# An attention and two MoE layers on one core: two tokens of a head share a transpose and a score product, K and V lie in chunks of 120 and 108 rows

## The chip, the core and the metric

The kernel runs on one NeuronCore of a Trainium2 chip. Its engines are TensorE (PE; its weight loads are listed apart as PEld), VectorE (DVE), ScalarE (ACT), GpSimd (POOL) and SyncE (SP), which here only issues transfers; sixteen DMA engines move data between HBM and SBUF. The metric is device time in microseconds (us).

## The reference, cut to what matters

```python
def _attn_ref(q, k, v):                      # (8, 8, 576, 64): batch, head, token, D
    k_p = k.reshape(B, H, Sp, 8, D).mean(axis=3)     # 576 tokens pooled by 8: 72 rows
    v_p = v.reshape(B, H, Sp, 8, D).mean(axis=3)
    scores = scale * np.matmul(q, k_p.transpose(0, 1, 3, 2))
    attn = softmax(scores)
    return np.matmul(attn, v_p)
def reference(...):
    x = attn_out.transpose(0, 2, 1, 3).reshape(4608, 512)
    x = _moe_ref(x, ...)     # noisy top-2 gate of 8 experts, 512 -> 1024 -> 512, relu
    return _moe2_ref(x, ...) # h = x @ w_in; (h - tanh(h)) @ w_out, 512 -> 2048 -> 512
```

All arrays are float32. Every token's row passes through the two MoE layers by itself, so any order of the rows serves inside the kernel, as long as noise and output use the same one.

## The kernel before, in words

The program has three stages, one after another on TensorE: attention (`attention`, about the first 210 us of the span), the experts (`moe`) and the last layer (`Moe2`). The two MoE stages run in float16 pairs.

Attention is written out by hand, in one order for every engine (there is no scheduler). The 4608 tokens make 36 tiles of 128; a pair of batches is 9 tiles, and the fifth of them lies across both. A loop of steps runs over the tiles, and step t holds one stage of several tiles, in this order: `st_exps(t)` (ACT, one exponential for each head, L1370), `st_norm(t - 1)` (DVE), `st_g(t - 4)` (DVE: the output row `xr`, L1430, and the gate's logits `lg`, L1438, both out of the PSUM tile `px`), `st_attT(t - 2)` (PE transposes, L1395, and ACT copies, L1396), `st_q(t + 2)` (PE transposes, L1344, and an ACT copy, L1346), `st_scores(t + 1)` (PE, L1354, and the DVE maximum `mx`, L1357), the work that prepares a batch (below), and `st_av(t - 3)` (PE, L1413, into `px`). Between them `tick` puts in DVE work of the gate. An engine runs its instructions in the order in which they are written. An f32 product or transpose counts as two PE instructions in the trace.

**Scores.** `st_q` transposes a tile's q two heads at a time: 64 values of one head and 64 of the next make the 128 columns. The block `kb` of a batch holds the pooled K, with rows 0 to 63 filled for even heads and 64 to 127 for odd ones and zero elsewhere, so that one product of 144 columns gives the scores of both heads.

**Pooling.** The 576 rows of a batch (8 heads of 72) lie in five chunks of 128, 128, 128, 96 and 96 rows, each row with its 8 tokens side by side. Three additions halve them (L1171: 4, 2, 1 tokens), then `kbd` (L1331) multiplies each chunk by `parity`, an identity whose columns are zeroed by the head's parity, and one ACT copy brings the result to `kb` (L1334).

**Output.** `st_av` multiplies the transposed weights by `vb`, which holds for each chunk up to three heads of 64 + 16 columns (V and V times the gate's weights). A PSUM bank of `px` takes four heads, so chunk 2, which holds rows of heads 3, 4 and 5, is split into a product of one head (80 columns) and one of two:

```python
for g, parts in enumerate((((0, 0, 2), (1, 0, 3), (2, 0, 1)), ((2, 1, 2), (3, 0, 2), (4, 0, 2)))):
    for i, (c, j, w) in enumerate(parts):
```

`st_g` reads both banks with one instruction for `xr` and one for `lg`.

**Transfers.** `load_q` (L1187) brings a tile's q, 1024 runs of 256 bytes, four tiles ahead. K and V of batches 0 and 1 come whole (`load_kv`, L1153); later ones in halves, of which the second is added on arrival by POOL's queue (`load_half`, L1163 and L1165). At the start DVE builds `parity` (L1220 to L1225) and small constants, and `warm` lets PE multiply zeros (L1200) so that its clock is up.

Of the kernel before, what the change touches and what calls it, by code (L numbers as in the profile page):

```python
# [37 lines left out]
def kernel(ctx, tc, q, k, v, w_gate, w_noise, noise, w1, w2, w_in, w_out, out):  # L38
# [57 lines left out]
    z.run(ctx)  # L96

# [561 lines left out]
class Moe2:  # L659
# [165 lines left out]
    def main(self, near):  # L825
# [225 lines left out]
        def L2(j, f, blocks=range(4)):  # L1051
# [9 lines left out]
            if f == KF - 1:  # L1061
                for i in blocks:
# [6 lines left out]
                    r = 128 * (4 * j + i)  # L1069
                    nc.sync.dma_start(self.out[r:r + 128, :], o)  # L1070
# [57 lines left out]
def attention(nc, tc, st, V):  # L1128
# [13 lines left out]
    KV = {}  # L1142


    cuts = (0, 128, 256, 384, 480, 576)
# [23 lines left out]
    def add(e, b, nm, n, c=slice(0, 5)):  # L1169
        a = KV[b, nm]  # L1170
        e.tensor_add(a[:, c, 0:n], a[:, c, 0:n], a[:, c, n:2 * n])  # L1171

    QL = {}
# [37 lines left out]
    KB = [one.tile([128, 2 * HP * SP], F32, name=f"kb{i}") for i in range(2)]  # L1211
    VB = [one.tile([128, 5, 3, D + 2 * E], F32, name=f"vb{i}") for i in range(2)]

    of = one.tile([128, 5, 4], F32, name="of")
    odd = one.tile([128, 5, 2], F32, name="odd")
    lt = one.tile([128, 5, 4], F32, name="lt")
    for c0, c1, step, base in ((0, 3, 128 - 2 * SP, 2 * SP), (3, 5, 96 - 2 * SP, cuts[3] - 4 * SP)):
        nc.gpsimd.iota(of[:, c0:c1], pattern=[[step, c1 - c0], [-SP, 4]], base=base, channel_multiplier=1,
                       allow_small_or_imprecise_dtypes=True)
# [17 lines left out]
    load_q(2)  # L1237
    load_kv(1, "k")
    load_kv(0, "v", each)
    load_q(3)  # L1240
    for w, o in ((w_gate, 0), (w_noise, E)):
        nc.sync.dma_start(wg[:, 0:H, o:o + E], w.rearrange("(h p) e -> p h e", p=64))
    load_kv(1, "v")
    nz = ep.tile([128, NT, E], F32, name="nz")
    for c in each:
        add(nc.vector, 0, "k", 4, slice(*c))
# [3 lines left out]
    nc.vector.memset(zero8, 0.0)  # L1250
# [7 lines left out]
    for c0, c1, base, step in ((0, 1, 0, 0), (1, 4, 56, -16), (4, 5, 48, 0)):  # L1258
# [8 lines left out]
    def prep_jobs(b, first=False):  # L1267
# [94 lines left out]
    def st_exps(t):  # L1362
# [8 lines left out]
        if t % 4 == 3:  # L1371
            SM[1] = sm, t0
# [436 lines left out]
```

## Time and profile before

| | |
|---|---|
| three runs | 1750.15, 1753.28, 1758.94 us (median 1753.28) |
| the profiled execution | 1757.43 us, of which its span 1755.6 |
| PE, DVE, ACT, POOL busy | 98%, 72%, 53%, 16% of the span |
| PE busy in 0 to 15, 15 to 30, 75 to 150, 150 to 210 us | 11.16 of 15, 10.37 of 15, 71.69 of 75, 57.47 of 60 us |
| DMA share in 45 to 60, 75 to 150, 150 to 210 us | 1.18, 1.00, 0.48 |

A DMA share is the mean busy share of the sixteen engines, where packets that overlap on an engine count twice. PE's busy time counts the whole length of a product, and lengths overlap, so a PE that is busy may still be waiting a little.

### The profile page before, as it was taken

The numbers are of one execution on the slowest core, as the hardware profiler recorded it, in microseconds if no ns is written. First come the engines' busy times: TensorE is split into PE (matmuls) and PEld (weight loads), VectorE is DVE, ScalarE is ACT, GpSimd is POOL, SyncE is SP. The second block draws the span as 40 slices with busy tenths as digits, with TensorE's granted clock in tenths as the row PEclk, the third lists the DMA queues.
The fourth block names the chain that finished last, engine by engine and source line by source line (L and its number), as shares of the span: only waits on it lengthen the run. The fifth ranks groups of instructions, "written<-read, shape, count | busy, mean of one in ns | idle before, by whom it ended". The sixth has DMA issues, their size and how long they took to land.

```text
span 1755.6 us, 28446 instructions
## 1 busy us (share of the span) xinstructions
PE 1723.1 (98%) x10574; PEld 1040.4 (59%) x10576; DVE 1266.2 (72%) x2547; ACT 922.9 (53%) x2229; POOL 274.7 (16%) x267
## 2 busy tenths in 40 slices
PE   7999999999999999999999999999999999999997
PEld 5989855454454545445454544666666666666664
DVE  5789788766666676666564558688787978888775
ACT  5788634435243443434343446656575756657553
POOL 2443113131030301101010211102010101200000
PEclk9999999999999999999999999999999999999999
DMA  9998335645746464535643445223131304232100
GB/s 222 271 192 214 103 106 165 165 132 150 184 124 181 137 175 132 126 120 131 170 131 88 124 125 127 68 53 85 43 87 35 97 19 97 66 50 64 22 25 26
DMA packets 271413, 203.35 MB, mean 116 GB/s; under 512 B 188512, under 2 KB 222816, under 8 KB 271264
## 3 DMA queue, kind: packets, MB, share of 16 engines
q1 hardware_dynamic: 251808, 155.09, 33.9%
q0 software_dynamic: 19200, 45.89, 11.4%
q8 instruction: 85, 1.39, 0.3%
q14 instruction: 64, 0.52, 0.1%
q10 hardware_dynamic: 256, 0.46, 0.1%
HBM read 121.82 MB, written 45.74 MB: 95 GB/s over the span
## 4 chain that ended last, share of the span: by engine, by line
PE 91%; DMA 3%; DVE 3%; ACT 2%; SPq 1%; issue 1%; ACTq 0%; DVEq 0%
PE pt L917 10%; PE ph L356 7%; PE ph L917 7%; PE ph L358 7%; PE ph L357 7%; PE py L1058 7%; PE py L1059 7%; PE py L1060 7%; PE py L378 7%; PE py L379 7%; PE py L380 7%; PE px L1413 3%; PE py L385 1%; PE psc L1354 1%; DMA qt<-in_q 1%; DMA xTp<-xp 1%
## 5 line engine op out<-in xcount | busy, mean ns | idle before, releaser
L360 ACT ACTIVATE hT<-ph 128x512 f16<-128x512 f32 (+2 forms) x192 | 96.4, 504 | 400.3 <-PE ph L358 390.6
L356 PE MATMUL ph<-xTp,pair 128*128 128x384 f16 (+2 forms) x736 | 245.4, 333 | 2.9 <-DMA xTp<-xp 2.9
L357 PE MATMUL ph<-xTp,pair 128*128 128x384 f16 (+2 forms) x736 | 244.9, 333 | 0.0
L358 PE MATMUL ph<-xTp,pair 128*128 128x384 f16 (+2 forms) x736 | 244.9, 333 | 0.0
L361 DVE SCALAR_TENSOR_TENSOR hT<-ph,hT 128x512 f16<-128x512 f32 (+2 forms) x192 | 110.6, 576 | 182.8 <-ACT hT L360 181.1
L1060 PE MATMUL py<-wo,gT 128*128 128x512 f16 x576 | 218.3, 379 | 1.2 <-DVE gT L1007 1.2
L1058 PE MATMUL py<-wo,gT 128*128 128x512 f16 x576 | 218.3, 379 | 0.0
L378 PE MATMUL py<-pair,hT 128*128 128x512 f16 x576 | 218.3, 379 | 0.0
L380 PE MATMUL py<-pair,hT 128*128 128x512 f16 x576 | 218.3, 379 | 0.0
L379 PE MATMUL py<-pair,hT 128*128 128x512 f16 x576 | 218.3, 379 | 0.0
L1059 PE MATMUL py<-wo,gT 128*128 128x512 f16 x576 | 218.3, 379 | 0.0
L917 PEld LDWEIGHTS <-wi 128*128 128x128 f16 x1536 | 150.2, 98 | 58.5 <-DMA y<-yp 0.3
L315 POOL DMA_INDIRECT xg<-x_d,idx x75 | 79.1, 1055 | 653.1 <-DVE xp L342 480.8
L730 POOL DMA_INDIRECT y<-y_d,ridx x64 | 79.2, 1238 | 518.6 <-DVE y L741 278.2
L356 PEld LDWEIGHTS <-pair 128*128 128x128 f16 x768 | 75.0, 98 | 75.7 <-issue 12.9
L358 PEld LDWEIGHTS <-pair 128*128 128x128 f16 x768 | 75.1, 98 | 56.5
L357 PEld LDWEIGHTS <-pair 128*128 128x128 f16 x768 | 75.1, 98 | 56.0 <-issue 0.2
L1017 ACT ACTIVATE th<-th,bias 128x512 f32<-128x512 f32 x144 | 102.5, 712 | 3.4 <-DVE th L1015 3.2
L1018 DVE SCALAR_TENSOR_TENSOR th<-th,t 128x512 f32<-128x512 f32 x144 | 98.3, 683 | 1.4 <-ACT th L1017 1.4
L1014 DVE SCALAR_TENSOR_TENSOR t<-hb,cinf,hs 128x512 f32<-128x512 f32 x64 | 47.9, 749 | 71.0 <-ACT hs L1013 71.0
L1007 DVE TENSOR_TENSOR gT<-th,gT 128x512 f16<-128x512 f32 x144 | 98.4, 683 | 0.2 <-ACT gT L1006 0.2
L1060 PEld LDWEIGHTS <-gT 128*128 128x128 f16 x576 | 56.3, 98 | 69.5 <-DVE gT L1007 1.7
(319 smaller groups left out, 3415.6 us busy)
## 6 DMA issues: line engine op xcount, KB each, us to landing
stage<-in_moe_w SPq DMA_DIRECT2D x64, 512.0 KB
y_d<-ys SPq DMA_DIRECT2D x82, 256.0 KB
x_d<-xr SPq DMA_DIRECT2D x36, 256.0 KB
out<-o SPq DMA_DIRECT2D x36, 256.0 KB
qt<-in_q SPq DMA_DIRECT2D x32, 256.0 KB
raw<-in_moe_w_in SPq DMA_DIRECT2D x32, 256.0 KB
raw<-in_moe_w_out SPq DMA_DIRECT2D x32, 256.0 KB
ws_d<-ys SPq DMA_DIRECT2D x16, 256.0 KB
```

Source lines behind the costliest of these rows:

```text
L356: nc.tensor.matmul(p[:, :nt], w[:, 0, m, s], x[:, 0, m, :nt], start=(m == 0), stop=False)
L357: nc.tensor.matmul(p[:, :nt], w[:, 0, m, s], x[:, 1, m, :nt], start=False, stop=False)
L358: nc.tensor.matmul(p[:, :nt], w[:, 1, m, s], x[:, 0, m, :nt], start=False, stop=(m == KD - 1))
L361: stt(h[:, 1, :nt], p[:, :nt], 0.0, h[:, 0, :nt], op0=OP.max, op1=OP.subtract)
L378: nc.tensor.matmul(p, h[:, 0, s], w[:, 0, f], start=(f == 0), stop=False)
L379: nc.tensor.matmul(p, h[:, 0, s], w[:, 1, f], start=False, stop=False)
L380: nc.tensor.matmul(p, h[:, 1, s], w[:, 0, f], start=False, stop=(f == KF - 1))
L917: nc.tensor.matmul(p, w[:, a, m], y[:, c, b, m], start=(start and m + x == 0), stop=(m == 1 and x == 2), skip_group_check=True)
L1017: nc.scalar.activation(q, q, AF.Square, bias=bias[:, 2:3], scale=SP5)
L1058: nc.tensor.matmul(p, g[:, 0, s], wo[:, 0, f], start=(f == 0), stop=False)
L1059: nc.tensor.matmul(p, g[:, 0, s], wo[:, 1, f], start=False, stop=False)
L1060: nc.tensor.matmul(p, g[:, 1, s], wo[:, 0, f], start=False, stop=(f == KF - 1))
```

## The change

Four things are changed, all in attention, with what they bring along at the two ends (the order of the tokens).

- **Tokens.** Four neighbouring tokens of a head are read as one run of 1024 bytes: partition p of a group holds tokens 4p to 4p + 3. Tiles 0 to 3 and 5 to 8 of each nine are such groups; tile 4 is read as before. So the tokens of a tile are now every fourth one of 512, and output rows (`token_rows`) and noise follow.
- **Scores.** A transpose takes two neighbouring tokens of one head instead of two heads of one token, and the product gives the scores of both tokens by that head's K. The even tile of a pair does heads 0 to 3 for both tokens, the odd tile heads 4 to 7; the weights of both tiles are complete after the second. `kb` now holds all heads twice, once in rows 0 to 63 and once in rows 64 to 127, with zeros that POOL writes once; ACT copies one half and DVE the other. `parity` is gone.
- **Chunks.** They have 120, 120, 120, 108 and 108 rows: 360 rows are five heads, so chunks 0 to 2 fill one bank with heads 0 to 4 and chunks 3 and 4 the other with heads 5 to 7. The product of one head is gone; `st_g` takes two instructions for `xr` and two for `lg`. Three chunks of a load now have 120 rows and two have 108.
- **Start.** The first K additions stand ahead of DVE's constants; V of batch 0 is loaded ahead of K of batch 1; fewer products of zeros; the first additions of batch 1 come one step later.

```diff
+def token_rows(a, t):
+    g, u = divmod(t, 9)
+    r = 1152 * g + (512 if u == 4 else 640 * (u > 4))
+    if u == 4:
+        return a[r:r + 128, :]
+    return a[r:r + 512, :].rearrange("(p i) d -> p i d", i=4)[:, u % 5, :]
...
-    cuts = (0, 128, 256, 384, 480, 576)
+    cuts = (0, 120, 240, 360, 468, 576)
...
-    def load_q(t):
-        qt = ld.tile([128, H, D], F32, name="qt", bufs=4)
+    def load_q4(t, h=slice(0, H), i=slice(0, 4)):
+        b, s = divmod(t * 128, S)
+        if t not in QG:
+            QG[t] = ld.tile([128, H, 4, D], F32, name="qt4", bufs=2)
+            for j in range(4):
+                QL[t + j] = QG[t][:, :, j]
+        nc.sync.dma_start(QG[t][:, h, i], q[b, h, s:s + 512, :].rearrange("h (p i) d -> p h i d", i=4)[:, :, i])
...
-    warm(22)
-    for nm in "kv":
-        for i in range(2):
-            nc.gpsimd.memset(KVT[nm][i][96:128, 3:5], 0.0)
+    warm(18)
     load_kv(0, "k", each, (nc.sync, nc.scalar))
-    load_q(0)
-    load_q(1)
+    load_q4(0, i=slice(0, 2))
+    KB = [one.tile([128, 20 * SP], F32, name=f"kb{i}") for i in range(2)]
+    for t in KB2:
+        nc.gpsimd.memset(t[64:128, 0], 0.0)
+        nc.gpsimd.memset(t[0:64, 1], 0.0)
+    def pads(nm, i):
+        nc.gpsimd.memset(KVT[nm][i][96:128], 0.0)
+    for nm, i in (("v", 0), ("k", 1), ("v", 1)):
+        pads(nm, i)
...
-    parity = one.tile([128, 5, 2, 128], F32, name="parity")
-    tt(parity, identf[:, None, None, :].to_broadcast([128, 5, 2, 128]), odd[:, :, :, None].to_broadcast([128, 5, 2, 128]), op=OP.mult)
+    for c in each:
+        add(nc.vector, 0, "k", 4, slice(*c))
...
-                        nc.tensor.matmul(p[64 * i:64 * i + 64, c - c0], KV[b, "k"][:w, c, 0], parity[:w, c, i, 0:w],
+                        nc.tensor.matmul(p[64 * i:64 * i + 64, c - c0], KV[b, "k"][:w, c, 0], identf[:w, 0:w],
                                          start=True, stop=True, skip_group_check=True)
-                o = KB[b % 2][:, cuts[c0]:cuts[c1]].rearrange("p (c n) -> p c n", n=w)
-                nc.scalar.activation(o, p, AF.Copy, scale=1.0 / 512)
+                o = KB2[b % 2][:, :, cuts[c0]:cuts[c1]].rearrange("p i (c n) -> p i c n", n=w)
+                nc.scalar.activation(o[0:64, 0], p[0:64], AF.Copy, scale=1.0 / 64)
+                ts(o[64:128, 1], p[64:128], 1.0 / 64, None, op0=OP.mult)
...
-                    nc.tensor.matmul(p[o:o + n, 2 * m:2 * m + 2].rearrange("p h s -> p (h s)"),
-                                     QT[t][:, 2 * g + m, o:o + n], KB[b % 2][:, 2 * SP * (2 * g + m):2 * SP * (2 * g + m + 1)], start=True, stop=True)
+                        h = SP * (HP * (t - a) + 2 * g + m)
+                        kb = KB2[b % 2][:, :, h:h + SP]
+                    nc.tensor.matmul(x, QT[t][:, 2 * g + m, o:o + n], kb, start=True, stop=True)
...
-        if t % 4 == 0:
-            SM[0] = wk.tile([128, 4, 2, 4], F32, name="sm"), t
+        if t % 9 in (0, 4, 5):
+            SM[0] = wk.tile([128, 4, H], F32, name="sm"), t
...
-            for g, parts in enumerate((((0, 0, 2), (1, 0, 3), (2, 0, 1)), ((2, 1, 2), (3, 0, 2), (4, 0, 2)))):
+            for c in range(5):
+                r, h, w = cuts[c + 1] - cuts[c], hb[c] - 5 * (c > 2), 2 + (c == 1)
+                nc.tensor.matmul(p[c > 2][o:o + n, n1 * h:n1 * (h + w)], a[:r, c, o:o + n],
...
+        for h, x, r in gs:
+            tt(xr.rearrange("p (h n) -> p h n", n=D)[:, h], x[:, :, 0:D], r.to_broadcast([128, x.shape[1], D]), op=OP.mult)
...
+    def load_nz():
+        n, o = noise.rearrange("(g s) e -> s g e", s=2 * S), nz.rearrange("p (g t) e -> p g t e", t=9)
+        for t, s in ((0, 0), (5, S + 64)):
+            for g in range(B // 2):
+                nc.sync.dma_start(o[:, g, t:t + 4], n[s:s + 512, g].rearrange("(p i) e -> p i e", i=4))
+        nc.sync.dma_start(o[:, :, 4], n[512:640])
...
-            load_q(t + 4)
+        for u, h in ((t + 6, slice(0, 4)), (t + 5, slice(4, 8))):
+            if 5 < u < NT and u % 9 in (0, 5):
+                load_q4(u, h)
+        if 4 < t + 4 < NT and (t + 4) % 9 == 4:
+            load_q1(t + 4)
...
-            warm((4, 2, 6, 4)[t])
+            warm((3, 0, 2, 0)[t])
```

DVE at the start of the program, before, from its first instruction after two constants down to the last addition of batch 0's K (`kt`):

```order
L1220 TENSOR_SCALAR lt<-of 128x20
L1221 TENSOR_SCALAR of<-of 128x20
L1222 TENSOR_TENSOR of<-of,lt 128x20
L1225 TENSOR_TENSOR parity<-identf,odd 128x1280
L1227 TENSOR_SCALAR before<-rowi 128x128
L1232 MEMSET idx 128x288
L1171 TENSOR_TENSOR kt_109<-kt_109 128x256 x5
L1250 MEMSET zero_202 128x8
L1453 MEMSET mb_213 128x44
L1171 TENSOR_TENSOR kt_109<-kt_109 128x5x128
L1171 TENSOR_TENSOR kt_109<-kt_109 128x5x64
```

and after, down to the first maxima (`mx`), the additions of batch 0's V (`vt`) and the first constant:

```order
L1182 TENSOR_TENSOR kt_109<-kt_109 120x256 x3
L1182 TENSOR_TENSOR kt_109<-kt_109 108x256 x2
L1182 TENSOR_TENSOR kt_109<-kt_109 120x3x128
L1182 TENSOR_TENSOR kt_109<-kt_109 108x2x128
L1182 TENSOR_TENSOR kt_109<-kt_109 120x3x64
L1182 TENSOR_TENSOR kt_109<-kt_109 108x2x64
L1344 TENSOR_SCALAR kb_141<-pt 64x360
L1344 TENSOR_SCALAR kb_141<-pt 64x216
L1386 TENSOR_REDUCE mx<-psc 128x4 x4
L1182 TENSOR_TENSOR vt_111<-vt_111 128x256 x5
L1182 TENSOR_TENSOR vt_111<-vt_111 128x5x128
L1182 TENSOR_TENSOR vt_111<-vt_111 128x5x64
L1292 TENSOR_REDUCE vm<-vt_111 128x1
L1272 TENSOR_SCALAR lm<-hm 128x15
```

The additions of K moved ahead of every constant (the constants now stand behind V's additions), `parity` with its four small steps is gone, and two DVE copies to `kb` stand between the additions and the first maxima.

SP's queue at the start, before, from the first loads of q (`qt`) on:

```order
L1187 DMA qt<-in_q 128x8x64 x3
L1153 DMA kt_110<-in_k 128x3x512
L1153 DMA kt_110<-in_k 96x2x512
L1153 DMA vt_111<-in_v 128x512 x3
L1153 DMA vt_111<-in_v 96x512 x2
L1187 DMA qt<-in_q 128x8x64
L1242 DMA wg<-in_moe_w_gate 64x8x8
L1242 DMA wg<-in_moe_w_noise 64x8x8
L1153 DMA vt_112<-in_v 128x3x512
L1153 DMA vt_112<-in_v 96x2x512
L1187 DMA qt<-in_q 64x8x64 x2
L1187 DMA qt<-in_q 128x8x64
```

and after:

```order
L1201 DMA qt_139<-in_q 128x8x128 x2
L1161 DMA vt_111<-in_v 120x512 x3
L1161 DMA vt_111<-in_v 108x512 x2
L1161 DMA kt_110<-in_k 120x3x512
L1161 DMA kt_110<-in_k 108x2x512
L1252 DMA wg<-in_moe_w_gate 64x8x8
L1252 DMA wg<-in_moe_w_noise 64x8x8
L1206 DMA qt<-in_q 64x8x64 x2
L1201 DMA qt_179<-in_q 128x8x256
L1161 DMA vt_112<-in_v 120x3x512
L1161 DMA vt_112<-in_v 108x2x512
```

Tiles 0 to 3 of q now come with the first two loads and tiles 5 to 8 in one (L1201), both ahead of the last V; V of batch 0 stands ahead of K of batch 1.

DVE in the step of tile 7, where K of batch 2 is copied to `kb`, before:

```order
L1171 TENSOR_TENSOR kt_109<-kt_109 128x5x64
L1430 TENSOR_TENSOR xr<-px,rc 128x512
L1438 TENSOR_TENSOR lg<-px,rc 128x128
L1357 TENSOR_REDUCE mx<-psc 128x4 x2
L1171 TENSOR_TENSOR vt_111<-vt_111 128x5x64
L1283 TENSOR_REDUCE vm<-vt_111 128x1
```

and after:

```order
L1182 TENSOR_TENSOR kt_109<-kt_109 128x5x64
L1460 TENSOR_TENSOR xr<-px,rc 128x320
L1460 TENSOR_TENSOR xr<-px,rc 128x192
L1467 TENSOR_TENSOR lg<-px,rc 128x80
L1467 TENSOR_TENSOR lg<-px,rc 128x48
L1386 TENSOR_REDUCE mx<-psc 128x4 x2
L1344 TENSOR_SCALAR kb_141<-pt 64x360
L1344 TENSOR_SCALAR kb_141<-pt 64x216
L1182 TENSOR_TENSOR vt_111<-vt_111 128x5x64
L1292 TENSOR_REDUCE vm<-vt_111 128x1
```

A tile has two instructions more (`xr` and `lg` by bank), and in the step that builds `kb` two copies stand behind the maxima.

## Rows read from the trace of the kernel before

**Rows 1.** The page: span, and busy time of each engine.

```profile
span 1755.6 us, 28446 instructions
...
PE 1723.1 (98%) x10574; PEld 1040.4 (59%) x10576; DVE 1266.2 (72%) x2547; ACT 922.9 (53%) x2229; POOL 274.7 (16%) x267
```

**Rows 2.** Four stretches: length, busy PE, PEld, DVE, ACT, POOL, PE clock, DMA share, GB/s.

```profile
15.00:30.00 15.00, 10.37 (x62) 7.90 (x61) 9.13 (x19) 10.43 (x55) 0.00 (x0) 0.89 1.03 233
14.84:36.34 21.50, 16.71 (x126) 13.40 (x127) 14.34 (x32) 14.47 (x77) 4.26 (x4) 0.92 1.09 214
75.00:150.00 75.00, 71.69 (x614) 67.17 (x613) 62.32 (x172) 63.02 (x293) 34.71 (x37) 0.98 1.00 223
61.00:210.00 149.00, 142.92 (x1206) 134.39 (x1207) 123.11 (x345) 120.75 (x561) 51.56 (x59) 0.99 0.81 192
```

**Rows 3.** Chain of waits, 0 to 61 us: start, length, what.

```profile
20.49 7.75 DMA qt<-in_q
...
48.37 12.74 DMA qt<-in_q
```

**Rows 4.** Waits of PE, 12 to 61 us: total, times, longest.

```profile
PE pt L1344 <- DMA qt<-in_q: 4.6, 2, 2.4
```

**Rows 5.** The same, 61 to 210 us.

```profile
PE pt L1344 <- DMA qt<-in_q: 1.4, 1, 1.4
```

**Rows 6.** Timeline, 0 to 12 us: start, length, engine, line.

```profile
6.89 1.49 DVE L1225 TENSOR_TENSOR parity<-identf,odd 128x1280 f32<-128x1280 f32 x1
...
8.91 1.71 DVE L1171 TENSOR_TENSOR kt<-kt 128x256 f32<-128x256 f32 x5
```

**Rows 7.** Timeline, 12 to 36 us.

```profile
12.12 1.21 PE L1331 MATMUL pt<-parity,kt 128*64 128x128 f32 x20 [2.61 <-DVE kt L1171]
...
14.14 1.15 PE L1354 MATMUL psc<-kb,qT 128*128 128x144 f32 x8
...
28.38 0.63 PE L1344 MATMUL pt<-identf,qt 128*128 128x128 f32 x4 [2.41 <-DMA qt<-in_q]
...
33.10 1.48 DVE L1171 TENSOR_TENSOR vt<-vt 128x1280 f32<-128x1280 f32 x1
...
35.39 0.95 DVE L1357 TENSOR_REDUCE mx<-psc 128x4 f32<-128x288 f32 x2 [0.81 <-PE psc L1354]
```

**Rows 8.** Chain of waits, 61 to 206 us: share of each line.

```profile
by line: PE px L1413 30.8%; PE psc L1354 11.4%; DMA qt<-in_q 8.8%; PE pt L1395 8.5%; ACT at L1370 8.0%; PE pt L1344 5.0%; PE pt L1303 4.3%; PE pt L1331 3.2%; DVE xr L1430 2.5%; DVE mx L1357 1.9%; issue 1.8%; ACT aT L1396 1.8%; PE pt L1539 1
```

**Rows 9.** Chain of waits, 144 to 168 us.

```profile
150.06 2.77 PE px L1413 x24
...
154.94 1.72 PE px L1413 x12
...
157.21 0.44 PE pt L1344 x4
...
164.67 1.24 PE pt L1303 x10
```

**Rows 10.** Timeline of DVE, 204.9 to 207 us: a tile whose banks are read apart.

```profile
205.11 0.75 DVE L1430 TENSOR_TENSOR xr<-psc,rc 128x256 f32<-128x256 f32 x2
205.78 0.34 DVE L1438 TENSOR_TENSOR lg<-psc,rc 128x64 f32<-128x64 f32 x2
```

**Rows 11.** Timeline of DVE, 103.5 to 104.5 us: a tile before.

```profile
103.61 0.69 DVE L1430 TENSOR_TENSOR xr<-px,rc 128x512 f32<-128x512 f32 x1 [0.50 <-PE px L1413]
104.22 0.28 DVE L1438 TENSOR_TENSOR lg<-px,rc 128x128 f32<-128x128 f32 x1
```

**Rows 12.** Groups of DVE, 0 to 220 us: count, busy, mean ns, idle before.

```profile
L1430 DVE TENSOR_TENSOR xr<-px,rc 128x512 f32<-128x512 f32 x34 | 23.4, 688 | 13.4 <-PE px L1413 12.6
```

**Rows 13.** Copies of ACT to `kb`, 0 to 220 us.

```profile
L1334 ACT ACTIVATE kb<-pt 128x384 f32<-128x384 f32 x8 | 3.9, 491 | 9.0 <-PE pt L1331 9.0
```

**Rows 14.** DMA, 30 to 150 us: packets, and the queue of SP.

```profile
DMA packets 46214, 28.27 MB, mean 236 GB/s; under 512 B 29833, under 2 KB 42230, under 8 KB 46198
...
q1 hardware_dynamic: 39818, 21.88, 71.2%
```

More of the change, by code (lines that the diff above doesn't have):

```diff
@@ L1170, in add @@
         a = KV[b, nm]
-        e.tensor_add(a[:, c, 0:n], a[:, c, 0:n], a[:, c, n:2 * n])
-    QL = {}
+        whole = (b, nm) != (0, "k")
+        for c0, c1 in [(c.start, c.stop)] if whole else [s for s in ((c.start, min(c.stop, 3)), (max(c.start, 3), c.stop)) if s[0] < s[1]]:
+            w = 128 if whole else cuts[c1] - cuts[c1 - 1]
+            e.tensor_add(a[:w, c0:c1, 0:n], a[:w, c0:c1, 0:n], a[:w, c0:c1, n:2 * n])
+    QL, QG = {}, {}
     def runs(t):
@@ L1209, in attention @@
+    for t in KB2:
+        nc.gpsimd.memset(t[64:128, 0], 0.0)
+        nc.gpsimd.memset(t[0:64, 1], 0.0)
+    VB = [one.tile([128, 5, 3, D + 2 * E], F32, name=f"vb{i}") for i in range(2)]
+    def pads(nm, i):
+        nc.gpsimd.memset(KVT[nm][i][96:128], 0.0)
+    for nm, i in (("v", 0), ("k", 1), ("v", 1)):
+        pads(nm, i)
     rowi = one.tile([128, 128], F32, name="rowi")
     nc.gpsimd.iota(rowi, pattern=[[1, 128]], base=0, channel_multiplier=-1, allow_small_or_imprecise_dtypes=True)
-    KB = [one.tile([128, 2 * HP * SP], F32, name=f"kb{i}") for i in range(2)]
@@ L1212, in attention @@
[L1212 to L1219, printed above, removed]
@@ L1236, in attention @@
     nc.gpsimd.iota(lane, pattern=[[0, 1]], base=0, channel_multiplier=1, allow_small_or_imprecise_dtypes=True)
-    load_q(2)
+    load_q4(0, i=slice(2, 4))
+    load_kv(0, "v", each)
     load_kv(1, "k")
-    load_kv(0, "v", each)
-    load_q(3)
     for w, o in ((w_gate, 0), (w_noise, E)):
         nc.sync.dma_start(wg[:, 0:H, o:o + E], w.rearrange("(h p) e -> p h e", p=64))
+    load_q1(4)
+    load_q4(5)
     load_kv(1, "v")
     nz = ep.tile([128, NT, E], F32, name="nz")
-    for c in each:
-        add(nc.vector, 0, "k", 4, slice(*c))
     head = ep.tile([128, NT, 2, 2], F16, name="head")
@@ L1257, in attention @@
     lm = one.tile([128, 5, 3], F32, name="lm")
-    for c0, c1, base, step in ((0, 1, 0, 0), (1, 4, 56, -16), (4, 5, 48, 0)):
+    for c0, c1, base, step in ((0, 1, 0, 0), (1, 4, cuts[1] - SP, cuts[1] - 2 * SP), (4, 5, cuts[4] - 6 * SP, 0)):
         nc.gpsimd.iota(hm[:, c0:c1], pattern=[[step, c1 - c0], [-SP, 3]], base=base, channel_multiplier=1,
@@ L1362, in st_exps @@
     def st_exps(t):
-        at = wk.tile([128, 2, 4, SP], F32, name="at", bufs=3)
-        if t % 4 == 0:
-            SM[0] = wk.tile([128, 4, 2, 4], F32, name="sm"), t
+        a = both_of(t)
+        if t % 9 in (0, 4, 5):
+            SM[0] = wk.tile([128, 4, H], F32, name="sm"), t
         sm, t0 = SM[0]
-        AT[t] = at
+        if a != t - 1:
+            for u in (t,) if a is None else (t, t + 1):
+                AT[u] = wk.tile([128, H, SP], F32, name="at", bufs=4)
         for g, (p, mx) in enumerate(SC.pop(t)):
             for j in range(4):
-                nc.scalar.activation(at[:, g, j], p[:, j], AF.Exp, bias=mx[:, j:j + 1], accum_out=sm[:, t - t0, g, j:j + 1])
-        if t % 4 == 3:
-            SM[1] = sm, t0
+                u, h = (t, 4 * g + j) if a is None else (a + j % 2, HP * (t - a) + 2 * g + j // 2)
+                nc.scalar.activation(AT[u][:, h], p[:, j], AF.Exp, bias=mx[:, j:j + 1], accum_out=sm[:, u - t0, h:h + 1])
+        if t % 9 in (3, 4, 8):
+            SM[1 + t] = sm, t0
     def st_norm(t):
-        if t % 4 != 3:
+        if t % 9 not in (3, 4, 8):
             tick(2)
             return
-        sm, t0 = SM.pop(1)
+        sm, t0 = SM.pop(1 + t)
+        sm = sm[:, 0:t + 1 - t0]
         ts(sm, sm, 1e-9, None, op0=OP.add)
         tick()
-        rc = wk.tile([128, 4, H], F32, name="rc")
-        nc.vector.reciprocal(rc, sm.rearrange("p t a b -> p t (a b)"))
+        rc = wk.tile([128, 4, H], F32, name="rc", bufs=3)[:, 0:t + 1 - t0]
+        nc.vector.reciprocal(rc, sm)
         for u in range(t0, t + 1):
@@ L1616, in attention, with consts @@
         at(0, add, nc.vector, 0, "v", 4, slice(*c))
+    at(0, pads, "k", 0)
     at(0, P[0]["v2"])
     at(0, P[0]["v1"])
+    def consts():
+        head_mask()
+        nc.vector.memset(wg[:, H:], 0.0)
+        ts(before, rowi, 0.0, None, op0=OP.is_gt)
+        nc.vector.memset(ones, 1.0)
+        nc.vector.memset(idx, 0)
+        nc.vector.memset(zero8, 0.0)
+        for m in mb:
+            nc.vector.memset(m, 0.0)
+    at(0, consts)
     at_pe(1, P[0]["vt"])
```

87 lines of the change are left out of this document (43 added, 44 removed).

## The prediction

> **What bounds the kernel now.** I read the page first: PE is busy for 98% of a span of 1755.6 us [rows 1], so a change pays only where PE waits or where PE's own work shrinks. The change touches attention, the first 210 us, and leaves the 1545 us behind it as they are; those are PE's, so that what attention gains or loses arrives at the end one for one. The profiled execution took 1757.43 us, 1.8 outside its span. The sum is made against it; the median of the three runs is 4.15 us (0.24%) lower, and the forecast is moved down by that.
>
> Next the stretches [rows 2]. From 61 to 210 us PE is busy 142.92 of 149 us, DVE 123.11 and ACT 120.75: PE leads, two others are close behind. From 14.84 to 36.34 PE has 16.71 of 21.5, DVE 14.34, ACT 14.47: nobody is full, all wait. For whom is in the chain of the first 61 us: a q load from 20.49 on (7.75 us) and another from 48.37 (12.74 us) [rows 3]. PE stood 4.6 us in two waits for q there [rows 4] and 1.4 in a third just after [rows 5]. The DMA share is 1.03 to 1.09 in these stretches and 1.00 from 75 to 150 us, but 0.81 over 61 to 210 [rows 2]. So the start is set by transfers and by DVE's order, the rest mostly by PE: in the later chain the product with V holds 30.8%, five more PE lines 32%, all exponentials 8.0% [rows 8].
>
> **The change part by part.**
>
> *First scores.* DVE builds `parity` from 6.89 on and comes to K's additions only at 8.91, where it then waits for nothing [rows 6]; PE gets the pooled K at 12.12 and the first scores run at 14.14 [rows 7]. With the constants behind them the additions can begin when K lands. That is between no gain and some 3 us: 2.0 from 6.89 to 8.91, and the small steps ahead of `parity`. The two copies to `kb` now stand one behind the other (DVE's waits for ACT's), about 0.5 us more [rows 13], and the first q load has 512 instead of 256 KB, at 233 GB/s [rows 2] 1.1 us more. I take 1.5 us: first scores at about 12.6.
>
> *Steps 0 to 4.* Before, step 2 stood until tile 4's q was there: its transposes ran at 28.38 [rows 7]. Now tiles 0 to 3 come with the first loads and tile 4 needs no place behind K and V of batch 1 and a third tile. Once q no longer holds, the engines' work does: 14.34 us of DVE between the first maxima (14.84) and those of tile 4 (end 36.34), to which the moved constants (1.5 us) and the copies to `kb` (0.8) come, and from which V's first addition of batch 1 goes, 1.48 us [rows 7], since it now stands behind tile 4's maxima. That makes 15.2 us; with some 3 us for PE and ACT, which have 14 to 17 us of their own in turn, 18. From 13.3 on this ends at 31.3, 5 us ahead. The postponed addition is still to be done, and DVE has room for it after step 4, so I count a gain of **4.5 us** for both parts (from 2, if K's landing and PE's clock hold it, to 7.5). The granted clock is 0.89 from 15 to 30 us [rows 2], where PE waits most; fifteen products of zeros less are a risk there, fewer waits the opposite.
>
> *Third wait for q.* A tile's q is 1024 runs of 256 bytes; SP's queue took 71.2% of sixteen engines for 120 us with 39818 packets, 34 ns each [rows 14], so a tile costs at most 2.2 us of all engines. As 256 runs of 1 KB at the mean 236 GB/s it costs 1.1. With a group loaded five steps ahead the third wait goes: **1.4 us** (0 to 1.4). 32 tiles save some 1 us each of transfer, which is worth nothing by itself: nothing else in the chain after 61 us is a transfer.
>
> *Product with V.* The one-head product goes, two PE instructions of 80 columns. A tile's twelve take 1.72 us for 960 columns [rows 9]; by columns the two are 0.14, by number 0.29. Transposes of 128 columns take 0.11 each (four in 0.44) and products of 48 columns 0.124 (ten in 1.24), so that a narrower one is no cheaper: I take 0.22 a tile. Tiles across two batches have 24 shorter ones in 2.77, so their parts lose 0.18. All in all 32 x 0.22 + 8 x 0.18 = 8.4 us of PE. After 61 us 30.8% of 145 us = 44.7 us of this product are on the chain, 26 tiles' worth, so at most 5.7 us. DVE and ACT are 20 us behind over 149, unevenly: in steps where one of them leads, PE's saving becomes a wait. I take **4.5 us** (2 to 6.7).
>
> *Two more DVE instructions a tile.* Read apart, two banks took from 205.11 to 206.12 [rows 10]; read together, from 103.61 to 104.50 [rows 11]: 0.12 more, at most 0.34 if each added one costs half of the pair's 0.34. Over 34 tiles 4.1 us. The first of them still waits for all five products, as the order of the program has it, so nothing begins earlier. DVE idles before this instruction anyway, 12.6 us in 34 tiles for the product with V [rows 12], and that covers it where PE leads. `xr` is 2.5% of the later chain, 3.6 us, five tiles; with PE faster it will be there more often: **1 us** lost (0.6 to 4; without the cover up to 11.6).
>
> *`kb` by DVE.* Two copies for a batch, some 0.8 us by the 0.69 us that 512 elements out of PSUM take [rows 11]. They wait for PE's products and for ACT's copy before them: ACT's own wait there is 9.0 us in 8 batches [rows 13], with its 0.49 us copy about 1.6. Behind them on DVE stand V's last addition, the gate's steps and the next tile's `xr`, which waits for PE in most steps. For six batches 14 us at worst, nothing at best; I take the copies of two batches, **1.5 us**. ACT's part is as long as before (as many elements in a row).
>
> *The rest.* Three more sums and reciprocals a kernel (a new one after 4, 1 and 4 tiles), 0.3 us. The scores have as many columns as before, the transposes too; 36 output stores keep 2 KB rows; nine noise loads instead of one pass SP's queue ahead of the q group for tile 9, which is needed four steps later. POOL's longer zero fills stand ahead of V's and the second K's loads, and I take them to be over when SP comes there. All that I cost at nothing.
>
> Sum: -4.5 - 1.4 - 4.5 + 1.0 + 1.5 + 0.3 = **-7.6 us**, 1749.8 for the profiled execution and 1745.7 against the median, 0.43% less. I take 0.5%, about 9 us, for what a measurement here can tell from no change.
>
> **The rivals.**
>
> *DVE becomes the bound (slower).* From 61 to 210 us it has 123.11 us of work [rows 2]. The added work is 29 x 0.12 + 6 x 0.8 + 1 = 9.3 us, the waits of the copies 6 x 1.6 = 9.6: 142, against PE's 142.92 less 6.7. If the copies' waits are not hidden, DVE leads in most steps, the saving of PE is lost and 14 to 18 us come instead: with the start's 5.9 us gained, some +10 us, 1763. It decides from the point at which a step's DVE work, wait included, passes PE's, about 4.7 us a tile. For it: DVE is in order, and the copy waits for an engine that has a step's work ahead of it. Against it: DVE idles 12.6 us before `xr`, and only six steps have the copies.
>
> [...]
>
> *More than forecast.* If first scores come the full 3 us earlier and the steps take what DVE has to do, the start gives 8 to 9 us; if PE stays the leader in each step, the product gives 6.7 and the DVE terms fall to 1: -14 us, 1739. For it: both losses lie in idle time that the trace shows.
>
> **How the numbers follow.** The forecast (1741 to 1750) gets 0.50, a little less than half of it beyond 0.5%; more than forecast 0.22; transfers still set the start 0.15; DVE the bound 0.13. So faster 0.45, same 0.42, slower 0.13. The range reaches from the best case with every term at its end (-15 us, and 2 us for the median of a few runs: 1736) to the second rival and some of the way to the first, 1757; what is left out is the first rival's end and a little below.
>
> **What would show it.** First scores near 12.6 us; no PE wait for q in the first 61 us; tile 4's maxima near 31 us; ten PE instructions for the product with V in about 1.5 us where PE leads; `kb` copies on DVE with a wait of 1 to 2 us for ACT; attention's last `xr` about 7 us earlier, and the rest as long as before. Wrong it would be by a granted clock below 0.9 in the start, by K and V landing later, or by DVE idle moving from `xr` into `kb`.

## The result, and the profile after

The changed kernel took 1765.83 us (median of 6 runs, 1761.05 to 1769.22) beside 1754.02 for the kernel before on the same chip: ratio 1.0070, 95% interval 1.0052 to 1.0089. It is slower by 0.7%, by the ratio 12.3 us (9.1 to 15.6), where 0.43% faster was forecast. The profiled execution took 1766.92 us, 1.8 outside its span.

The page of the changed kernel, span and busy time of each engine (to be held against [rows 1]):

```profile
span 1765.1 us, 28281 instructions
...
PE 1723.4 (98%) x10481; PEld 1037.4 (59%) x10481; DVE 1274.9 (72%) x2634; ACT 922.7 (52%) x2229; POOL 286.0 (16%) x269
```

PE has 93 matmuls less and is busy as long as before. The work behind attention is as before; up to the last tile's transposed weights in attention (`aT` of tile 35, at 221.73 us here and 206.01 before) PE is busy 189.15 us at a mean granted clock of 0.95, where it was 188.45 at 0.98: what was taken out came back as time in which the same work ran slower. Where, the stretches say (length, busy PE, PEld, DVE, ACT, POOL, PE clock, DMA share, GB/s; the second runs from the first maxima to those of tile 4):

```profile
15.00:30.00 15.00, 10.65 (x78) 8.43 (x77) 12.93 (x40) 10.34 (x55) 0.00 (x0) 0.89 0.95 223
13.12:32.59 19.47, 15.12 (x116) 12.03 (x115) 15.01 (x44) 14.32 (x76) 1.36 (x1) 0.91 0.96 225
45.00:60.00 15.00, 10.54 (x80) 8.87 (x79) 6.29 (x19) 8.21 (x42) 6.26 (x6) 0.90 1.11 289
75.00:150.00 75.00, 63.91 (x490) 58.37 (x490) 57.45 (x173) 53.00 (x242) 30.94 (x33) 0.91 0.90 195
61.00:210.00 149.00, 130.74 (x1022) 119.86 (x1022) 123.75 (x373) 111.30 (x527) 54.06 (x59) 0.94 0.78 184
```

The start came near the forecast: the stretch from the first maxima to tile 4's is 19.47 us long instead of 21.50; it begins 1.72 us sooner and ends 3.75 us sooner [rows 2], where 5 were forecast for its end. The loss lies behind it. From 75 to 150 us PE, DVE and ACT are all less busy than before, by 8, 5 and 10 us, and the PE clock is 0.91 instead of 0.98 [rows 2]. All three waiting more suggests that something outside them is late. The DMA share fell too, from 1.00 to 0.90, and the GB/s from 223 to 195, so that the transfers look less loaded than before. That is the row that misleads here, as the experiments show.

The chain of waits of the changed kernel, 0 to 61 us, and under it from 61 to 100 (start, length, what):

```profile
7.72 6.05 DMA vt<-in_v
...
22.98 11.37 DMA vt<-in_v
...
44.24 11.15 DMA x_d<-xr
```

```profile
67.25 3.27 SPq L1206
...
70.57 9.76 DMA qt<-in_q
```

Before, two loads of q stood in the first 61 us [rows 3]. Now it is V twice, then the store of tile 0's x, which took 11 us to land and which `xr` of tile 3 waits for (three buffers). Behind 61 us stands the load of q for tile 13, the tile without a neighbour (`load_q1`, L1206; called the lone query below): it stands 3.27 us on SP's queue and takes 9.76 us to land.

PE's waits, 12 to 61 us, and under them 61 to 226 us (total, times, longest):

```profile
PE px L1445 <- DVE lg L1467: 5.1, 2, 3.2
...
PE pt L1366 <- DMA qt<-in_q: 1.2, 1, 1.2
```

```profile
PE pt L1366 <- DMA qt<-in_q: 3.7, 1, 3.7
```

The waits for q in the start fell from 4.6 to 1.2 us [rows 4], the third one grew from 1.4 to 3.7 [rows 5]. The 5.1 us ahead of the product with V are put down to DVE's `lg`, but DVE itself stands 6.1 us for a store ahead of `xr` (its groups are shown further down).

Three lines of the chain behind 61 us are the product with V of one tile, ten instructions at 3 us; here the windows of just these:

```profile
101.08:104.11 3.03, 3.03 (x11) 2.85 (x12) 2.08 (x6) 1.46 (x10) 3.03 (x6) 0.53 0.02 5
132.15:135.16 3.01, 3.01 (x11) 2.84 (x11) 0.48 (x2) 0.09 (x1) 3.01 (x4) 0.50 0.43 47
194.02:196.99 2.97, 2.97 (x13) 2.80 (x12) 1.08 (x6) 0.67 (x5) 0.00 (x0) 0.53 0.00 0
```

The granted clock is 0.50 to 0.53. PE had waited 0.74, 1.66 and 2.18 us, until 1.6, 4.0 and 1.1 us before. If the wait is what lowers the clock, as the order in time suggests and no run tried, it is paid twice here: once standing, and once more, about 1.5 us (3.0 where 1.50 is measured at a clock of 1.00, below), in the tile behind it. The last tile's `aT` (the start of ACT's first copy to it) comes at 221.73 us instead of 206.01; the time from there to the end is 6 us shorter than before, of which 2.9 is a wait of PE for a transfer (`xTp`) between 440 and 485 us, and 2.9 the longer landing of the last store, both in this execution of before. Such times of `aT`, here and below, are those of one execution of each kernel; executions of one kernel differ by up to some 10 us.

### The profile page after: what moved, and what is told of

It reads as the page before. It is cut to its first block, busy times and chain, and to the rows that moved or that the text cites. A ratio compares the mean times of both kernels' runs of the same rounds, so it can differ in the third digit from the quotient of the medians.

```text
span 1765.1 us, 28281 instructions
## 1 busy us (share of the span) xinstructions
PE 1723.4 (98%) x10481; PEld 1037.4 (59%) x10481; DVE 1274.9 (72%) x2634; ACT 922.7 (52%) x2229; POOL 286.0 (16%) x269
## 4 chain that ended last, share of the span: by engine, by line
PE 89%; DVE 4%; DMA 3%; ACT 1%; SPq 1%; issue 1%; POOL 1%; another core or an unknown queue 0%; POOLq 0%; DVEq 0%; ACTq 0%
PE pt L926 10%; PE ph L365 7%; PE ph L367 7%; PE ph L366 7%; PE ph L926 7%; PE py L1067 7%; PE py L1069 7%; PE py L1068 7%; PE py L387 7%; PE py L389 7%; PE py L388 7%; PE px L1445 2%; PE py L394 1%; DMA vt<-in_v 1%; PE psc L1384 1%
```

## The experiments

Theory A: the loads of 120 and 108 rows (called narrow) land late, and all that stands behind them; that fewer DMA engines carry them is the author's guess at the cause, and no trace here shows which engines carry a load. Theory B: SP's queue is held by groups of queries (loads of q) and nine noise loads, and stores and queries land late (B': by the order in which the lone query is issued). Theory C: VectorE, with `xr` and `lg` split and the copies to `kb`, has become the bound. D came later: the transfers as a whole bound attention. All ratios are to the kernel before, run beside each kernel; the medians come from several chips, so differences between versions are taken from the ratios. Step 5 is the time from tile 5's `aT` to tile 6's. In all versions with wide loads, the maximum of V takes in a few rows more, as the expectation of the first one says.

**Tokens alone.** The changed kernel with `cuts = (0, 128, 256, 384, 480, 576)` and the `st_av` and `st_g` of before.

```diff
-    cuts = (0, 120, 240, 360, 468, 576)
+    cuts = (0, 128, 256, 384, 480, 576)
```

> The changed kernel with the old chunks (128, 128, 128, 96, 96 rows), the old product with V and the joint xr and lg: the two tokens that share a transpose, the groups of queries, the nine noise loads and POOL's fills stay. Theory A (loads of 120 and 108 rows land late because fewer DMA engines carry them) expects all that was lost after tile 4 to be gone: 1740 to 1748 us, and the loads of V at the start landing about 2 us sooner. Theory B (SP's queue: groups of queries and nine noise loads ahead of the stores of x, which land late) expects the loss to stay: 1762 to 1768, step 5 still about 12 us long. Theory C (the split xr and lg make VectorE the bound) expects 1750 to 1756, with steps 5 and 9 still long.

1754.17 us, ratio 1.0001 (0.9986 to 1.0016). The loss is gone, as A has it, but the gain that A expected with it (1740 to 1748) isn't there. Tile 5's `aT` comes at 45.73 us, 8.0 ahead of the kernel before; one step, tile 9 to 10, then takes 10.56 us instead of 5.36. In its chain, 45 to 82 us:

```profile
57.07 4.13 SPq L1206
61.24 9.77 DMA qt<-in_q
```

It is the lone query of tile 13 again, without any narrow load. So there are two causes.

**Chunks alone.** The kernel before with the new cuts, `st_av`, `st_g`, zero fills, bases of the masks and the first K's additions by chunk length.

```diff
-    cuts = (0, 128, 256, 384, 480, 576)
+    cuts = (0, 120, 240, 360, 468, 576)
...
-            p = [p[:, 0], p[:, 1], p]
+            p = [p[:, 0], p[:, 1]]
```

> The kernel before with the chunks of 120 and 108 rows, one bank for each chunk in the product with V and the split xr and lg; transposes, queries, noise and the order of the loads stay as before. Theory A expects the loss here: 1762 to 1770, transfers of V at the start and the accumulating loads of K and V landing late. Theory B expects the forecast gain of the product with V less the split: 1747 to 1752. Theory C expects 1758 to 1765, with the product with V waiting on the lg group in most tiles.

1766.69 us, ratio 1.0068 (1.0045 to 1.0091): the whole loss, as A expected. Its chain from 40 to 62 us shows what a late transfer does:

```profile
33.65 16.31 DMA qt<-in_q
...
50.09 1.09 PE pt L1349 x4
51.18 1.92 PE psc L1359 x8
```

Tile 4's q, issued at 33.65 us, lands 16.31 us later; the four transposes then take 1.09 us and the eight scores 1.92, where 0.44 [rows 9] and 0.98 (the same eight in many other steps) are usual. The window 45 to 60 us has a PE clock of 0.58. The loads of q are not narrow; they stand behind those that are.

**Wide loads.** The changed kernel with 128 rows in each load for a chunk of 120 and 112 for one of 108, by a source whose chunks overlap; only the last batch's chunks 3 and 4, behind which no rows are left, keep 108.

```diff
+    def wide(rows, b, c0, c1):
+        n = 128 if c1 == 3 or c0 < 3 else 112 if b < B - 1 else 108
+        s = rows[cuts[c0]:cuts[c1]]
+        w = cuts[c1] - cuts[c1 - 1]
+        return n, bass.AP(s.tensor, s.offset, [[512, n], [512 * w, c1 - c0]] + [list(x) for x in s.ap[1:]])
...
-            w = cuts[c1] - cuts[c1 - 1]
-            engs[i % len(engs)].dma_start(a[:w, c0:c1], rows[cuts[c0]:cuts[c1]].rearrange("(c p) r d -> p c r d", p=w))
+            w, src = wide(rows, b, c0, c1)
+            engs[i % len(engs)].dma_start(a[:w, c0:c1], src)
```

> The changed kernel in which each load of K and V brings 128 rows for a chunk of 120 and 112 rows for one of 108 (the rows beyond a chunk are its neighbour's and reach no product; the maximum of V that sets its scale then covers up to four rows of the next batch). Theory A expects the bytes over 16 DMA engines to land sooner though there are 5% more of them: 1745 to 1753 us, step 5 at 7 us instead of 12. Theory B and theory C expect no change: 1762 to 1768.

1753.84 us, ratio 0.9999 (0.9984 to 1.0014): more bytes, and by the ratios 12 us less than the changed kernel. Step 5 takes 9.38 us instead of 12.23, not the 7 that A expected; but the profiled execution, 1759.74 us, is the slowest of the twelve. In it the store of tile 0's x still takes 10.95 us to land, so that the narrow loads are not what makes this store slow. The first three stretches of the changed kernel (two of them; 15 to 30 us stands above), and under them all three with wide loads:

```profile
0.00:15.00 15.00, 11.50 (x68) 6.52 (x68) 5.39 (x15) 4.58 (x14) 13.49 (x23) 1.00 0.90 223
...
30.00:45.00 15.00, 13.06 (x107) 12.20 (x108) 9.65 (x28) 13.00 (x72) 6.01 (x5) 1.00 0.97 172
```

```profile
0.00:15.00 15.00, 12.08 (x70) 7.08 (x72) 5.72 (x16) 5.09 (x18) 13.51 (x23) 1.00 0.95 267
15.00:30.00 15.00, 12.17 (x96) 9.80 (x95) 12.98 (x41) 11.69 (x64) 0.00 (x0) 0.89 1.10 279
30.00:45.00 15.00, 14.79 (x114) 14.01 (x111) 12.23 (x37) 14.62 (x78) 6.73 (x5) 1.00 1.05 198
```

The DMA share is a mean over 16 engines. With narrow loads it stays at 0.90 to 0.97 and the rate at 223, 223 and 172 GB/s; with wide ones it is 0.95 to 1.10 and 267, 279 and 198. The rates differ by 1.20 and 1.25 in the first two stretches. So the lower share of the changed kernel, 0.90 to 0.97, did not mean that its transfers had room; whether some engines had a full queue while others had nothing is not shown, since the share of a single engine stands in no trace here.

The semaphore events in the trace (counted for each load; the last of them is taken as its landing) differ with the rows:

| load | rows | events | first event after the issue | first to last |
|---|---|---|---|---|
| K of batch 0, changed kernel, 0.75 us | 120 | 16 | 0.58 us | 3.68 us |
| the same, 1.45 us | 108 | 13 | 0.48 | 5.25 |
| K of batch 0, wide loads, 0.75 us | 128 | 16 | 3.14 | 0.87 |
| the same, 1.67 us | 112 | 16 | 4.86 | 0.95 |
| uneven cut (below), 1.25 us | 20 | 11 | 0.46 | 3.18 |

The wide loads have 16 events, the first of them 3.14 and 4.86 us after the issue and all within 1 us. Each of the three narrow ones has an event 0.46 to 0.58 us after its issue; with 120 rows 15 more follow, with 108 rows 12 and with 20 rows 10, and the last comes 3.18 to 5.25 us after the first. The second halves that POOL's queue adds on arrival have 16 events with 120 and 108 rows too, the first never sooner than 2.59 us after the issue. So the events of loads from SP and ACT go with the number of rows, and those of loads from POOL do not. How many engines a load runs on the events do not tell.

**Six buffers of `xr`.** `name="xr", bufs=6` in the changed kernel.

> The changed kernel with six buffers of xr instead of three, so that xr of tile 3 no longer waits until the store of tile 0 has landed. Theory B expects the chain's 11 us from that store to the next xr to go: step 5 falls from 12.2 us to about 7, and the time to 1755 to 1761. Theory A expects that the wait is only one of several behind late transfers and another takes its place: 1761 to 1767, step 5 still over 10 us. Theory C expects no change: 1763 to 1768.

1762.51 us, ratio 1.0047 (1.0028 to 1.0065), which overlaps the changed kernel's interval: some 4 us may be in it, and it stays unclear. Step 5 still takes 10.15 us. The wait for the store is gone from the chain, and from 48 to 72 us another transfer is in its place, a load of V:

```profile
48.43 10.66 DMA vt<-in_v
```

That is theory A's expectation for this run: most of the loss is not the store's.

**Noise late.** `at(8, load_nz)` instead of `at(2, load_nz)` in the changed kernel.

> The changed kernel (narrow loads and all) with the nine loads of noise issued at step 8 instead of step 2. Theory A (narrow loads) expects 1762 to 1768, no change, since the narrow loads of K and V for batch 2 land late all the same. Theory B (the nine loads ahead of queries and stores on SP's queue) expects that the product with V of tiles 4 and 5 comes 3 us sooner and 1757 to 1762 in all.

1762.98 us, ratio 1.0049 (1.0031 to 1.0068). Some 4 us may be in it; the intervals overlap, so it stays unclear, and most of the loss stays.

**Wide loads and the lone query early.** It is issued one step sooner, ahead of the next group's halves.

```diff
+        if 4 < t + 5 < NT and (t + 5) % 9 == 4:
+            load_q1(t + 5)
         for u, h in ((t + 6, slice(0, 4)), (t + 5, slice(4, 8))):
             if 5 < u < NT and u % 9 in (0, 5):
                 load_q4(u, h)
-        if 4 < t + 4 < NT and (t + 4) % 9 == 4:
-            load_q1(t + 4)
```

> The changed kernel with 128 and 112 rows in each load of K and V, and in it the query of the tile that has no neighbour (tiles 13, 22, 31) issued one step earlier, ahead of the next group's loads instead of behind them. With wide loads alone it took 1753.84 us, 8 above the forecast. Theory B' (order on SP's queue: this query stands behind 1 MB of a group that is needed later; in the profiles with and without the wide loads the transposes of queries wait 3.4 to 3.9 us between 60 and 120 and 2.1 to 2.9 between 120 and 180) expects about 5 us back: 1747 to 1751. Theory D (the transfers as a whole bound this stage: DMA share 1.05 to 1.13 from 15 to 75 us, so whatever TensorE saves comes back as another wait) and theory C (VectorE bounds it) expect 1752 to 1755.

1750.88 us, ratio 0.9975 (0.9962 to 0.9988): by the ratios 4.2 us (0.7 to 7.7) under wide loads alone, and faster than the kernel before. The step from tile 9 to 10 falls from 9.56 to 5.33 us, and no wait of PE for a load of q is left from 61 to 120 us; the costliest there is

```profile
PE pt L1314 <- ACT aT L1434: 2.4, 2, 1.7
```

where wide loads alone had

```profile
PE pt L1371 <- DMA qt<-in_q: 2.5, 1, 2.5
```

That is what B' expected. D in its strict form, by which nothing comes back, is refuted.

**The fourth corner.** The changed kernel with its narrow loads and the early lone query.

> The changed kernel with its narrow loads (120 and 108 rows) and the lone query issued early: the fourth corner beside the changed kernel (1765.8), wide loads (1753.8) and both (1750.9). Theory A (the loads' width has a price of its own, about 12 us) expects 1759 to 1764. If the order on SP's queue were the cause and the width only made it worse, 1750 to 1754.

1761.81 us, ratio 1.0050 (1.0034 to 1.0066). The width costs 0.0071 with the late query (1.0070 to 0.9999) and 0.0075 with the early one (1.0050 to 0.9975); the query 0.0020 and 0.0024. Each of these differences is known to some 0.0020 to 0.0024; within that the two add up.

**Two more edits on top.** Wide loads and the early query, the noise in three loads and six buffers of `xr`; and tokens alone with the same three edits of the queues.

> As the run with wide loads and the early lone query, and besides the noise in three loads instead of nine and six buffers of xr. Theory B' expects the forecast: 1743 to 1748. Theory D expects 1751 to 1755 still. Theory C expects 1750 to 1755, with VectorE's product lg ahead of the product with V in the waits.

> Tokens alone (the old chunks, product with V, and joint xr and lg, which took 1754.17 us) with the early lone query, the noise in three loads and six buffers of xr. Theory B' expects 1745 to 1750. Theory D expects 1752 to 1755. Theory C expects this one 3 us or more below the run with wide loads and the same three edits, since xr and lg are joint here; without C it should be 3 to 4 us above that run, for the longer product with V.

1751.77 us, ratio 0.9985 (0.9973 to 0.9997), and 1750.38, ratio 0.9975 (0.9961 to 0.9989). Without narrow loads, neither noise nor stores show a price any more: theory B falls but for the lone query, and the first of the two misses the 1743 to 1748 of B'. It lies in the ranges of C and D, so that what keeps the version with chunks some 3 us above the forecast is not shown. And tokens alone are no slower than tokens with chunks, though their product with V is longer: the product's saving does not show.

**Chunks with wide loads; the split alone.** The kernel of chunks alone with the wide loads, and the kernel before with only `p = [p[:, 0], p[:, 1]]`, which makes `xr` and `lg` two instructions each.

> Chunks alone (1766.7 us) with 128 and 112 rows in each load of K and V. Theory A expects the 12 to 13 us back: 1752 to 1756. With the forecast's gain of the product with V less its split on top it would be 1749 to 1751; if theory C holds, the split takes that gain and it stays at 1753 to 1756.

> The kernel before with xr and lg of every tile split over the two banks (four heads each), nothing else. The forecast priced this at 1.0 us, 0.12 us of VectorE for a tile and little of it on the path: 1754 to 1756. Theory C expects 3 to 5 us more than before: 1757 to 1760.

1754.05 us, ratio 1.0006 (0.9995 to 1.0017), and 1756.58, ratio 1.0014 (1.0002 to 1.0026). The split costs 2.5 us (0.4 to 4.6). Chunks without narrow loads, split included, are worth +1.1 us (-0.9 to 3.0). The difference, -1.4, give or take 3, is what the product with V brought, if the split by five and three heads costs what this one by four and four does and the wide loads' extra bytes cost nothing.

**The split taken out.** Wide loads, the early query, and each head's output at 103 columns: heads 0 to 4 end at column 492 of the first bank, head 5 begins at 515, in the second, and one access pattern takes all eight.

```diff
-            p = [p[:, 0], p[:, 1]]
+            p = [p.rearrange("p g n -> p (g n)")[:, 0:8 * 103].rearrange("p (h n) -> p h n", n=103)]
...
+                    y, x = p[0][o:o + n, hb[c]:hb[c] + w, 0:n1], vb[:r, c, 0:w]
```

> Wide loads and the early lone query (1750.9 us), and the product with V laid out with one head each 103 columns, so that heads 0 to 4 lie in the first bank, 5 to 7 in the second, and xr and lg are one instruction each again for all tiles but 33 and 35. Theory C (the split xr and lg on VectorE eat the gain of the shorter product with V) expects 1746 to 1749. If the split is worth only the 1 us of the forecast or is covered, 1749 to 1752.

1748.90 us, ratio 0.9970 (0.9957 to 0.9984), the lowest ratio of all. By the ratios it is 0.9 us under the version with the split (0.9970 against 0.9975), well within the intervals, so that C is neither shown nor refuted in its small form; its large one (VectorE eats everything) is refuted. In the profiled execution, at 1745.15 us the fastest of the twelve, `aT` of tile 35 comes at 199.84 us, 6.2 before that of the kernel before, with a granted clock of 1.00 over the span. Up to there PE does its 1442 instructions in 176.51 us of busy time; the changed kernel takes 189.15 for as many, at 0.95.

**Do the rows of a load alone do it?** The kernel before, each load of K and V in two. Uneven: 108 and 20, 72 and 24 rows. Even: 112 and 16, 80 and 16.

```diff
+    parts = {128: 108, 96: 72}
...
+            for p0, p1 in ((0, parts[w]), (parts[w], w)):
+                engs[i % len(engs)].dma_start(a[p0:p1, c0:c1], src[p0:p1])
```

> The kernel before, each load of K and V in two: 108 and 20 rows of the 128, 72 and 24 of the 96. [...] Theory A expects 12 us or more over the even cut of the companion run: 1766 to 1785. If only the number of rows in a load or the number of loads mattered, both would come out alike.

> The kernel before, each load of K and V in two: 112 and 16 rows of the 128, 80 and 16 of the 96, so that the number of loads and the bytes are those of the uneven cut but every load divides by 16. Theory A expects only the price of twice as many loads on SP's and POOL's queues: 1753 to 1760. If the number of loads is what costs, 1766 or more, as in the uneven cut.

1764.89 us, ratio 1.0057 (1.0038 to 1.0075), and 1756.59, ratio 1.0012 (0.9999 to 1.0026). Same bytes, same number of loads: the uneven rows cost 0.0045, 8 us, give or take 4; twice as many loads cost 2 us (-0.2 to 4.6). A's direction is right; its size, 12 us or more, is at the upper end of what was measured, and why it is not larger stays open. PE's waits for q from 0 to 215 us, uneven (an execution of 1774.58 us, the slowest of its eight) and then even:

```profile
PE pt L1348 <- DMA qt<-in_q: 19.1, 8, 4.6
```

```profile
PE pt L1348 <- DMA qt<-in_q: 7.1, 3, 3.0
```

Again it is the q loads, whose rows are the same in both, that come late.

## Why the prediction was wrong, step by step

**First scores at about 12.6 us.** Right, at 12.35. The timeline of the changed kernel, 11.5 to 12.9 us, and a row of 30.5 to 33 us (start, length, engine, line):

```profile
11.67 0.83 DVE L1344 TENSOR_SCALAR kb<-pt 64x360 f32<-64x360 f32 x2 [1.97 <-ACT kb L1343]
...
12.35 0.73 PE L1384 MATMUL psc<-kb,qT 128*128 128x144 f32 x4
```

```profile
31.64 0.95 DVE L1386 TENSOR_REDUCE mx<-psc 128x4 f32<-128x288 f32 x2 [1.40 <-PE psc L1384]
```

**Steps 0 to 4.** Near: tile 4's maxima run from 31.64 on and are done at 32.59, where "this ends at 31.3" was forecast. That it came so near is in part luck, for two errors offset each other: at tile 5's `aT` the changed kernel leads by 4.5 us, and with wide loads by 8.2. The start gains what "More than forecast" gave it (8 to 9), and the narrow loads take 3.7 of it back. Tokens alone, with the lone query early (and two edits that brought nothing elsewhere), gain 4.4 us (1.9 to 6.8); the terms of that half sum to -4.1 (-4.5, -1.4, +1.5, +0.3).

**"Nothing else in the chain after 61 us is a transfer."** This sentence failed: in the sum the narrow loads stand at nothing, and the runs show 12.5 us. It was true of the kernel before and was read as room, though the same rows have a DMA share of 1.00 from 75 to 150 us [rows 2]. It was no room: 12 us were lost when the loads of K and V became narrow (1.0070 less 0.9999). The chance that transfers still set the start, 0.15, was the nearest to it and looked at the start alone. It is the author's estimate, and no run shows a term for it; what the runs showed is 12.5 us, some 3.7 of it by tile 5. In the traces the lag does not end at the start. By the last semaphore event of each, in the changed kernel and with wide loads, K of batch 0 lands at 7.98 and 7.48 us, V of batch 0 at 17.12 and 14.89, K of batch 1 at 22.95 and 19.28, V of batch 1 at 34.35 and 29.47, and the first half of V of batch 2 at 39.43 and 33.32: 4.9 us for the four loads, 6.1 with the next, and K and V are loaded for most of attention (the last of their loads is issued at 161.2 us in the changed kernel). It falls on loads of q that are not narrow (PE's waits for q in the two cuts above: 19.1 against 7.1 us), and waits of PE are followed by work at the low clock, as in the three tiles above. The price should have been looked for over the whole time in which K and V are loaded: the share is between 0.89 and 1.18 in every 15 us of the kernel before up to 165.

**Third wait for q gone, -1.4.** Wrong. "With a group loaded five steps ahead the third wait goes" overlooked the tiles that belong to no group: 13, 22 and 31 are loaded four steps ahead, behind the second half of a group that is needed later. Early issue brought 4.2 us (0.7 to 7.7). The order in which a step issues its loads was there to read.

**Product with V, -4.5.** Mis-sized. A tile's ten take 1.50 us where twelve took 1.72 [rows 9], as forecast; here in the chain with wide loads and the early query, 156 to 186 us (the second of the three lines is a tile at the low clock, a mean of 0.63 in its window):

```profile
164.82 2.14 POOL vb L1337 x3
...
177.25 2.52 PE px L1450 x10
...
182.40 1.50 PE px L1450 x10
```

But of the 4.5 us the runs show 1.4, give or take 3. In the kernel with the first two repairs, the saving at the start (8.6 us at tile 5) shrinks to 1.5 at tile 35; the steps to tiles 27 and 29 take 8.10 and 8.97 us instead of 7.06 and 5.95. There the chain goes over DVE, POOL's scaling of V and ACT; that these are the bound there is read from the chain and was not tried. A part of it goes with the clock: with the two further edits of the queues, at a granted clock of 1.00 from 171 to 180.2 us, the step to tile 29 takes 7.33 us.

**Split `xr` and `lg`, +1.0 (0.6 to 4).** 2.5 (0.4 to 4.6) by itself. The groups of DVE in the changed kernel, 0 to 225 us (count, busy, mean ns, idle before):

```profile
L1460 DVE TENSOR_TENSOR xr<-px,rc 128x320 f32<-128x320 f32 x34 | 16.5, 487 | 15.1 <-PE px L1445 8.3 <-DMA x_d<-xr 6.1
L1460 DVE TENSOR_TENSOR xr<-px,rc 128x192 f32<-128x192 f32 x34 | 11.8, 348 | 0.0
```

487 and 348 ns stand for one of 688 [rows 12]. Of the idle time for PE ahead of it, counted as cover, 8.3 us are left of 12.6; another 6.1 are a wait for a store.

**`kb` by DVE, +1.5.** The wait for ACT was forecast at 1 to 2 us a batch. The first one is 1.97 (above), but only three of the eight batches have one, 3.4 us in all. ACT's copies take 463 and 343 ns where they took 491 and 325, so that its part is as long as before, as forecast. No run has the copies alone, so their price stays open.

**"The rest ... at nothing."** The noise loads: unclear in the changed kernel, no price once the loads are wide. That the part after attention stays as long as before held but for the 6 us of waits in this execution of before.

Summed: -7.6 forecast, +12.5 for narrow loads, +4.2 for the lone query, +3.1 for the product and +1.5 for the split give +13.7; measured were +12.3 (9.1 to 15.6). **DVE the bound**, the one rival on the slower side, had the right sign and the wrong mechanism; that its 1763 lies so near the measured 1765.83 is luck.

## What to carry to other kernels

Choose the rows of a load by when such loads land, not only by what the matrix product wants: here 120 and 108 rows cost 12 us of 1754, and bringing 128 and 112, useless rows included, took it back. Where the DMA share is near 1, as it was here (1.00 from 75 to 150 us), do not take a hidden transfer to have slack: price a cost on it over the whole stage and on everything queued behind it. In a change of several parts, read the order in which each step issues its loads, the odd tiles' above all.

## What the runs showed of the hardware

- A load of K or V issued from SP or ACT has 13 semaphore events with 108 rows, 16 with 120 and 11 with 20, and for K of batch 0 the first of them comes 0.46 to 0.75 us after the issue. With 112 and 128 rows, in K of batch 0 with wide loads, it has 16, the first 4.86 and 3.14 us after the issue; with 128 and 96 rows, in the kernel before, 16, the first 3.06 us or more after the issue. Loads of 120 and 108 rows from POOL's queue, in the changed kernel, have 16, the first 2.59 us or more after the issue.
- The mean DMA share at 15 to 30 us was 1.10 with wide loads and 0.95 with narrow ones, though the narrow ones landed later (V of batch 0 at 17.12 us, with wide loads at 14.89).
- After a load of q that took 16.31 us to land, eight scores took 1.92 us instead of 0.98, with a PE clock of 0.58 over 45 to 60 us, in a step of 13.74 us.
- As many PE instructions, 1442, kept PE busy for 176.51 us at a granted clock of 1.00 and for 189.15 at 0.95.
